# Two blocks' attention results turned on PE and ACT, and an earlier due time for the first weights in the order

## The chip, the cores and the metric

The kernel runs on one core of one Trainium2 chip. The metric is the device time of one execution in microseconds (us), the median of several executions. Engines, as the profile names them: PE is TensorE (matmuls and transposes; PEld is its weight load), DVE is VectorE, ACT is ScalarE, POOL is GpSimd, and SP is SyncE, which here only issues transfers (DMAs). Each engine runs its own list of instructions strictly in order and waits on semaphores for the others. The lists are fixed when the program is built.

## The reference

Chunked attention on 4 batches, 8 heads and 768 tokens, then a mixture of 8 experts whose mixing weights are balanced by eight Sinkhorn rounds:

```python
for c in range(nc):                       # 24 chunks of 32 queries
    # keys: 8 memory keys, and the chunk with 16 before and 8 behind it
    scores = scale * q_c @ k_full.T
    a = exp(scores - max(scores)); a = a / (sum(a) + 1e-9)
    out[:, :, chunk] = a @ v_full
x = out.transpose(0, 2, 1, 3).reshape(3072, 512)
logits = x @ w_gate; P = exp(logits - logits.max())
for _ in range(8):
    P /= P.sum(1) + 1e-9;  P /= P.sum(0) + 1e-9;  P *= N / E
for e in range(8):
    out += P[:, e] * (maximum(x @ w1[e], 0) @ w2[e])    # w1: 512x1024, w2: 1024x512
```

## The kernel before

Attention and experts are one program. The 3072 tokens are cut into 24 **blocks** of 128 tokens; attention works block by block, and two blocks make one of the groups of 256 tokens on which the expert matmuls run. For block n, `scores` has PE turn queries and keys (tq L1014, tk L1018, tx L814 for the rest of the context's keys), multiply them (sp L1077), DVE take the row maximum and subtract it (sm L1091, s L1097) and ACT the exponential (s L1116). `values` has PE turn the exponentials (ta L1134), ACT copy them to SBUF (at L1153), and PE multiply them with the values (xp L1144; the values carry a column of ones, so the row sum comes along). Then DVE divides (`share`: rec L1162 and L1163, xq L1165 twice), and turns the result so that features lie on the partitions (`turn_out`, STREAM_TRANSPOSE L1185, in squares of 32 by 32). The turned result xg is the input x of the experts.

The expert matmuls are done with pairs of 16-bit numbers. Every operand is scaled by a power of two that is found from its largest magnitude, and split into a high part (ACT, L518) and the rest (DVE, L526). So before the first expert matmul can start there is a **chain of scales**: the maxima of the values for x (vmax L982) and of the weights (mxs L562) on DVE, most_of L450, a transpose on PE (row_x and row_w, L499), a few tiny instructions on DVE (L507, L455, L456), PE again (sp_x, sp_w L486), DVE again (sx, sw L462), and then the splits. The first expert's first-layer weights w1f come in four tiles of 512 KB (`fetch_first`, `load` L553), the second layer's w2f too. The first unit of work uses plain products (pp L2046 for the first layer, yp L2127 for the second, h L2088 between them); all later ones use a Strassen form with sums of operands (px, py, pz, yx, yy, yz at L1599; the sums ws L606 and xt L1291 to L1315 on POOL or DVE; the intermediate sums c at L1668).

**What sets the order.** Every piece of work is a `Task` with an engine, a cost and a due time. `Plan` runs a list schedule over all of them when the program is built: it keeps a clock for each engine, takes the task that can start first, and emits its instructions in that order. A transfer is counted as landed at the end of its share of a common transfer clock, plus 2.6. So the numbers of the plan decide only the order; the chip then waits for what really comes last. Where the plan thinks that PE would be idle for more than 0.4 us it puts in matmuls without a result, named **warm** (L432, each 128x256), about as many as fill 0.8 of the gap. PSUM is cut into banks in groups ("att", "two", "main" and others); a task that `takes` a bank waits in the plan until one of its group is free.

## Time and profile before

| | |
|---|---|
| median of 3 runs | 1910.08 us (1908.98 to 1910.18) |
| profiled execution | 1910.83 us |
| its span in the trace | 1908.8 us |
| PE busy | 1898.1 us (99%) |
| DVE busy | 1466.2 us (77%) |
| ACT busy | 1022.9 us (54%) |
| POOL busy | 541.4 us (28%) |
| granted PE clock | 1.00 |

The profiled execution took 2.0 us more than its span, the time around it. In the views below a row of the timeline has the start, the length (of the whole group, where several are merged), the engine, the line, the operation, what it writes and reads, and in brackets how long the engine sat idle before it and who ended that. A row of the windows view has a stretch, its length, and for each engine its busy time and number of instructions.

### The profile page before, as it was taken

Reading aid. Unit: us, or ns where it says so; the run is one execution under the profiler, and the core shown is the slowest. Engines: PE = TensorE matmul, PEld = TensorE weight load, DVE = VectorE, ACT = ScalarE, POOL = GpSimd, SP = SyncE. Lnnn points to the kernel's source line nnn. Section 1 sums busy time; section 2 is a strip of 40 time slices with the busy share of each in tenths; the row PEclk is TensorE's granted clock in tenths of the full one; section 3 lists DMA queues with packets and bytes.
Section 4 is the critical chain, followed back from the end, with each engine's and each line's share of the span. In section 5 each row is a group of like instructions: output and inputs, shape, how many; then the busy total and the mean of one; then the engine's idle time right before and its main releaser. Section 6 shows DMA issues by size and latency. Waiting matters only on the chain.

```text
span 1908.8 us, 47094 instructions
## 1 busy us (share of the span) xinstructions
PE 1898.1 (99%) x19544; PEld 1635.1 (86%) x19544; DVE 1466.2 (77%) x2456; ACT 1022.9 (54%) x1999; POOL 541.4 (28%) x605
## 2 busy tenths in 40 slices
PE   9999999999999999999999999999999999999999
PEld 7777676788888888888888888888888888888888
DVE  6886679878589867898669876897778985786565
ACT  4765555556465545546445544655555563564453
POOL 4321112513134211522224231442124231332112
PEclk9999999999999999999999999999999999999999
DMA  9887653543324441264224433245313632322321
GB/s 212 199 217 167 169 168 126 168 166 106 128 78 161 150 142 70 90 222 160 84 95 160 156 122 112 89 160 183 123 45 115 247 109 100 95 84 85 127 84 67
DMA packets 207254, 254.81 MB, mean 133 GB/s; under 512 B 106208, under 2 KB 140128, under 8 KB 202688
## 3 DMA queue, kind: packets, MB, share of 16 engines
q1 hardware_dynamic: 203044, 249.17, 40.7%
q0 software_dynamic: 2080, 2.18, 0.6%
q8 instruction: 153, 2.51, 0.6%
q10 hardware_dynamic: 1916, 0.46, 0.2%
q14 instruction: 61, 0.50, 0.1%
HBM read 187.84 MB, written 63.44 MB: 132 GB/s over the span
## 4 chain that ended last, share of the span: by engine, by line
PE 97%; DVE 2%; issue 0%; ACT 0%; POOL 0%; DVEq 0%; POOLq 0%; ACTq 0%
PE px L1599 26%; PE yx L1599 23%; PE pz L1599 13%; PE yz L1599 11%; PE py L1599 6%; PE yp L2127 6%; PE yy L1599 6%; PE pp L2046 1%; PE xp L1144 1%; PE sp L1077 1%; PE warm L432 1%; PE ta L1134 1%; PE tk L1018 1%; PE tq L1014 0%; DVE w L526 0%; PE lp L1400 0%
## 5 line engine op out<-in xcount | busy, mean ns | idle before, releaser
L1599 PEld LDWEIGHTS <-w 128*128 128x128 f16 x7896 | 771.3, 98 | 93.9 <-issue 2.1
L1599 PEld LDWEIGHTS <-h 128*128 128x128 f16 x7056 | 690.4, 98 | 81.1 <-issue 0.9
L1599 PE MATMUL px<-x,w 128*128 128x256 f16 x4512 | 548.3, 273 | 0.6 <-DVE c L1668 0.5
L1932 POOL TENSOR_TENSOR acc<-acc,y 128x256 f32<-128x256 f32 x252 | 263.7, 1054 | 879.1 <-ACT y L1907 866.4
L1599 PE MATMUL yx<-w,h 128*128 128x256 f16 x4032 | 467.9, 273 | 0.5 <-DVE acc L1942 0.5
L1658 ACT ACTIVATE q<-px 128x256 f32<-128x256 f32 x376 | 143.1, 382 | 289.1 <-PE px L1599 284.2
L1599 PE MATMUL pz<-x,w 128*128 128x256 f16 x2256 | 278.1, 273 | 0.0
L1599 PE MATMUL yz<-w,h 128*128 128x256 f16 x2016 | 233.8, 273 | 0.0
L1827 DVE TENSOR_TENSOR h<-ss,h 128x1024 f16<-128x1024 f32 x168 | 217.7, 1299 | 3.6 <-ACT h L1803 3.6
L1778 ACT ACTIVATE h<-c 128x768 f16<-128x768 f32 x168 | 140.8, 838 | 111.6 <-DVE c L1668 111.6
L1803 ACT CAST h<-ss 128x1024 f16<-128x1024 f32 x168 | 174.1, 1039 | 38.5 <-DVE ss L1767 38.5
L1767 DVE SCALAR_TENSOR_TENSOR ss<-c,ss 128x256 f32<-128x256 f32 x336 | 176.4, 525 | 8.6
L1811 DVE SCALAR_TENSOR_TENSOR h<-c,h 128x768 f16<-128x768 f32 x168 | 168.2, 1004 | 9.2 <-ACT h L1778 9.1
L1668 DVE SCALAR_TENSOR_TENSOR c<-px,q 128x256 f32<-128x256 f32 x188 | 77.7, 421 | 96.6 <-PE px L1599 90.7
L1907 ACT ACTIVATE y<-yx,pscale 128x256 f32<-128x256 f32 x168 | 79.6, 474 | 120.6 <-PE yx L1599 116.5
L1599 PE MATMUL py<-x,w 128*128 128x256 f16 x1128 | 139.0, 273 | 0.6 <-DVE c L1668 0.6
L2127 PE MATMUL yp<-w,h 128*128 128x512 f16 x576 | 132.2, 379 | 0.5 <-DVE h L2088 0.5
L1767 DVE SCALAR_TENSOR_TENSOR ss<-c,h 128x512 f32<-128x512 f32 x168 | 125.0, 744 | 1.9 <-ACT h L1755 1.9
L1668 DVE SCALAR_TENSOR_TENSOR c<-py,q 128x256 f32<-128x256 f32 x188 | 78.4, 421 | 61.1 <-PE py L1599 56.5
L1599 PE MATMUL yy<-w,h 128*128 128x256 f16 x1008 | 116.9, 273 | 0.0
L2127 PEld LDWEIGHTS <-h 128*128 128x128 f16 x576 | 55.5, 99 | 58.9 <-DVE h L2088 1.0
L518 ACT ACTIVATE w<-ws,sw 128x1024 f16<-128x1024 f32 (+1 forms) x64 | 69.4, 1089 | 65.6 <-POOL ws L606 65.5
(165 smaller groups left out, 1775.1 us busy)
## 6 DMA issues: line engine op xcount, KB each, us to landing
x<-xkeep SPq DMA_DIRECT2D x28, 1792.0 KB
akeep<-acc SPq DMA_DIRECT2D x168, 256.0 KB
acc<-akeep SPq DMA_DIRECT2D x168, 256.0 KB
w1f<-in_moe_w_dram SPq DMA_DIRECT2D x36, 512.0 KB
w2f<-in_moe_w_dram SPq DMA_DIRECT2D x32, 512.0 KB
w1fm<-in_moe_w_dram SPq DMA_DIRECT2D x28, 512.0 KB
w2fm<-in_moe_w_dram SPq DMA_DIRECT2D x28, 512.0 KB
xkeep<-x SPq DMA_DIRECT2D x6, 1792.0 KB
```

The costliest lines, as they stand in the source:

```text
L518: lambda: nc.scalar.activation(dst(0), src(), AF.Copy, scale=s),
L1599: nc.tensor.matmul(dst.t, a, b, start=(not more and n == 0), stop=(n == end), skip_group_check=more,)
L1658: lambda: nc.scalar.activation(t.t, src.t, AF.Copy, scale=DOWN),
L1668: lambda: nc.vector.scalar_tensor_tensor(c.t[:, o], src.t, DOWN, q.t, op0=ALU.mult, op1=ALU.add),
L1767: lambda: nc.vector.scalar_tensor_tensor(dst(), src(), 0.0, other(), op0=ALU.max, op1=op),
L1778: lambda: nc.scalar.activation(h.t[:, 0, 0:3], c.t, AF.Relu),
L1803: lambda: nc.scalar.copy(h.t[:, 0, 3:7], ss.t),
L1811: lambda: nc.vector.scalar_tensor_tensor(h.t[:, 1, 0:3].rearrange("p a n -> p (a n)"), c.t.rearrange("p a n -> p (a n)"), 0.0, h.t[:, 0, 0 ...
L1827: lambda: spare.tensor_tensor(h.t[:, 1, 3:7], ss.t, h.t[:, 0, 3:7], op=ALU.subtract),
L1907: (lambda: nc.scalar.activation(t.t, src.t, AF.Copy, scale=f))
L1932: lambda: nc.gpsimd.tensor_tensor(acc.t[:, cols], acc.t[:, cols], q.t, op=ALU.add),
L2127: nc.tensor.matmul(py.t, hf.t[:, hl, where[fh], o : o + P], room(fp, WIDE * wl + DM * fh, WIDE * wl + DM * (fh + 1)), start=(fp == 0 and i ...
```

## The change

Two things. First, for blocks 0 and 1 the turn is moved from DVE to PE and ACT: `share` writes xq in another layout (the multiply is of the form 128x4x4x16 in place of 128x16x16, still twice), PE does four 128x128 transposes into a bank of the group "att" (xt), and ACT copies them to xg. For xq to come out so, xp is written with chunk and head pair exchanged. All other blocks stay as they were. Second, a task can have a `lead`, which is taken off the landing time that the plan counts for its transfer; the four loads of w1f have 3.8, all others 0.

```diff
+LEAD = 3.8
...
-                t.end = max(dma, at + t.cost) + 2.6
+                t.end = max(dma, at + t.cost) + 2.6 - t.lead
...
-        return st, add(eng, 1, go, after, prio, [st], dma=2.1)
+        return st, add(eng, 1, go, after, prio, [st], dma=2.1, lead=lead)
...
+        by_pe = n < 2
...
+                        m, j = (c, i) if by_pe else (i, c)
                         nc.tensor.matmul(
-                            xp.t[i * CH : (i + 1) * CH, par, c * DV : (c + 1) * DV],
+                            xp.t[m * CH : (m + 1) * CH, par, j * DV : (j + 1) * DV],
...
-        xq = buf("at", att, [P, CB, KT, CH], F32, f"xq_{n}")
+        xq = buf("at", att, [P, KT, P] if by_pe else [P, CB, KT, CH], F32, f"xq_{n}")
...
+                if by_pe:
+                    nc.vector.tensor_tensor(
+                        xq.t.rearrange("p k (i a f) -> p i k a f", a=2, i=HP)[:, :, :, a],
+                        x[:, a, :, 0:D].rearrange("p i (f k) -> p i k f", k=KT),
+                        r[:, a, :, None, None].broadcast_to([P, HP, KT, D // KT]),
+                        op=ALU.mult,
+                    )
+                    continue
...
-        t = add("DVE", 0.73, turn_out, [t], at + 2, [xq, gt])
+        if by_pe:
+            tx = bank("att", [P, KT, QB], f"xt_{n}")
+
+            def go_x():
+                for i in range(KT):
+                    nc.tensor.transpose(tx.t[:, i], xq.t[:, i], ident)
+
+            t = add("PE", 0.5, go_x, [t], at + 2, [xq, gt], takes=tx)
+            t = add(
+                "ACT",
+                0.6,
+                lambda: nc.scalar.copy(gt.t[:, :, o : o + QB], tx.t),
+                [t],
+                at + 2,
+                [gt],
+                frees=tx,
+            )
+        else:
+            t = add("DVE", 0.73, turn_out, [t], at + 2, [xq, gt])
...
-            st, ld = load(0, fp, which, FIRST[which - 1] + 0.5 * fp)
+            st, ld = load(0, fp, which, FIRST[which - 1] + 0.5 * fp, lead=LEAD if which == 1 else 0.0)
```

Since the plan schedules all tasks together, both edits move far more than the two blocks. Apart from line numbers and buffer numbers, the orders differ from the start up to work that ran at about 190 us before, and are the same from there on: the last 2024 of some 2270 rows of DVE, the last 30120 of some 32040 of PE, the last 1773 of ACT, 527 of POOL and 536 of SP agree. SP's first 54 rows, with the loads of w1f among them, agree too.

The first place is DVE at the start, from its first vmax to the last maximum of w1f. Blocks 0 and 1 are the first and second group of rec, xq; names end in a buffer's number. Before:

```order
L982 TENSOR_REDUCE vmax<-v_pair 128x1
L1162 TENSOR_SCALAR rec_425<-xp_390 128x8
L1163 RECIPROCAL rec_425<-rec_425 128x8
L1165 TENSOR_TENSOR xq_428<-xp_390,rec_425 128x16x16 x2
L1185 STREAM_TRANSPOSE xg_471<-xq_428 128x4x128
L1091 TENSOR_REDUCE sm_474<-sp_436 128x2x4
L1097 TENSOR_TENSOR s_477<-sp_436,sm_474 128x2x4x64
L982 TENSOR_REDUCE vmax<-v_pair 128x1
L562 TENSOR_REDUCE mxs<-w1f_0_290 128x1
L562 TENSOR_REDUCE mxs<-w1f_1_330 128x1
L1162 TENSOR_SCALAR rec_559<-xp_524 128x8
L1163 RECIPROCAL rec_559<-rec_559 128x8
```

After:

```order
L983 TENSOR_REDUCE vmax<-v_pair 128x1
L563 TENSOR_REDUCE mxs<-w1f_0_290 128x1
L1166 TENSOR_SCALAR rec_464<-xp_390 128x8
L1167 RECIPROCAL rec_464<-rec_464 128x8
L1170 TENSOR_TENSOR xq_467<-xp_390,rec_464 128x4x4x16 x2
L1092 TENSOR_REDUCE sm_473<-sp_431 128x2x4
L1098 TENSOR_TENSOR s_485<-sp_431,sm_473 128x2x4x64
L983 TENSOR_REDUCE vmax<-v_pair 128x1
L563 TENSOR_REDUCE mxs<-w1f_1_330 128x1
L563 TENSOR_REDUCE mxs<-w1f_2_340 128x1
L1166 TENSOR_SCALAR rec_559<-xp_524 128x8
L1167 RECIPROCAL rec_559<-rec_559 128x8
```

The maximum of w1f's first tile now stands ahead of block 0's rec, so DVE can't begin to divide block 0's result until that tile has landed; the other maxima stand earlier too, three of the four ahead of block 1's rec, and both STREAM_TRANSPOSE rows are gone.

The second place is DVE where the first Strassen unit begins (in the trace of before from 104 to 115 us): x is the unit's input split, w_0_2 and w_0_3 are the last two weight tiles' splits, c the unit's first intermediate sums, s the scores of a later block. Before:

```order
L526 SCALAR_TENSOR_TENSOR x_1996<-xg_1795,sx,x_1996 128x256
L526 SCALAR_TENSOR_TENSOR x_1996<-xt_1_2013,sx,x_1996 128x4x256
L526 SCALAR_TENSOR_TENSOR w_0_2_685<-ws_0_2_1884,sw,w_0_2_685 128x768
L1668 SCALAR_TENSOR_TENSOR c_1_0_2096<-py_1_0_2085,q_0_1_0_2072 128x256
L1097 TENSOR_TENSOR s_2100<-sp_1936,sm_1986 128x2x4x64
L1431 COPY lg<-lq_1975 128x32
L1668 SCALAR_TENSOR_TENSOR c_1_1_2119<-py_1_1_2102,q_0_1_1_2077 128x256
L562 TENSOR_REDUCE mxs<-w1fm_0_1835 128x1
L1091 TENSOR_REDUCE sm_2171<-sp_2121 128x2x4
L1097 TENSOR_TENSOR s_2184<-sp_2121,sm_2171 128x2x4x64
L526 SCALAR_TENSOR_TENSOR w_0_3_750<-ws_0_3_2098,sw,w_0_3_750 128x256
L1668 SCALAR_TENSOR_TENSOR c_1_0_2096<-px_1_0_2055,q_0_1_0_2197 128x256
```

After:

```order
L527 SCALAR_TENSOR_TENSOR x_2023<-xg_1827,sx,x_2023 128x256
L527 SCALAR_TENSOR_TENSOR x_2023<-xg_1462,sx,x_2023 128x256 x2
L527 SCALAR_TENSOR_TENSOR x_2023<-xg_1827,sx,x_2023 128x256
L527 SCALAR_TENSOR_TENSOR w_0_3_751<-ws_0_3_2017,sw,w_0_3_751 128x256
L527 SCALAR_TENSOR_TENSOR w_0_3_751<-ws_0_3_2017,sw,w_0_3_751 128x768
L1098 TENSOR_TENSOR s_2108<-sp_1930,sm_1967 128x2x4x64
L527 SCALAR_TENSOR_TENSOR x_2023<-xt_0_2019,sx,x_2023 128x4x256
L1698 SCALAR_TENSOR_TENSOR c_1_0_2124<-py_1_0_2095,q_0_1_0_2093 128x256
L1461 COPY lg<-lq_2002 128x32
L527 SCALAR_TENSOR_TENSOR x_2023<-xt_1_2082,sx,x_2023 128x4x256
L1698 SCALAR_TENSOR_TENSOR c_1_1_2189<-py_1_1_2110,q_0_1_1_2103 128x256
L1092 TENSOR_REDUCE sm_2199<-sp_2149 128x2x4
```

The two splits of w_0_3 and the scores s have moved ahead of the split of the sum xt_0, and that split ahead of the unit's first c on DVE; before, w_0_3 stood behind the first maximum w1fm.

The third place is POOL ahead of the same unit: the sums ws of the weight tile w_0_3 and the sums xt of the unit's input. Before:

```order
L606 TENSOR_TENSOR ws_0_2_1884<-w1f_2_1336,ws_0_2_1884 128x256
L798 DMA kx_1811<-in_k_dram 32x8x64
L1299 TENSOR_TENSOR xt_0_1993<-xg_1795 128x256
L1291 TENSOR_TENSOR xt_1_2013<-xg_1795,xg_1432 128x256
L1299 TENSOR_TENSOR xt_1_2013<-xg_1795 128x256
L1307 TENSOR_TENSOR xt_1_2013<-xg_1795,xt_1_2013 128x256
L1315 TENSOR_TENSOR xt_1_2013<-xg_1432,xt_1_2013 128x256
L606 TENSOR_TENSOR ws_0_3_2098<-w1f_3_1453 128x256
L606 TENSOR_TENSOR ws_0_3_2098<-ws_0_3_2098,w1f_3_1453 128x256
L606 TENSOR_TENSOR ws_0_3_2098<-w1f_3_1453 128x256
L606 TENSOR_TENSOR ws_0_3_2098<-w1f_3_1453,ws_0_3_2098 128x256
```

After:

```order
L607 TENSOR_TENSOR ws_0_2_1900<-ws_0_2_1900,w1f_2_1322 128x256
L607 TENSOR_TENSOR ws_0_2_1900<-w1f_2_1322 128x256
L607 TENSOR_TENSOR ws_0_2_1900<-w1f_2_1322,ws_0_2_1900 128x256
L607 TENSOR_TENSOR ws_0_3_2017<-w1f_3_1459 128x256
L607 TENSOR_TENSOR ws_0_3_2017<-ws_0_3_2017,w1f_3_1459 128x256
L607 TENSOR_TENSOR ws_0_3_2017<-w1f_3_1459 128x256
L607 TENSOR_TENSOR ws_0_3_2017<-w1f_3_1459,ws_0_3_2017 128x256
L1329 TENSOR_TENSOR xt_0_2019<-xg_1827 128x256
L1321 TENSOR_TENSOR xt_1_2082<-xg_1827,xg_1462 128x256
L1329 TENSOR_TENSOR xt_1_2082<-xg_1827 128x256
L1337 TENSOR_TENSOR xt_1_2082<-xg_1827,xt_1_2082 128x256
L1345 TENSOR_TENSOR xt_1_2082<-xg_1462,xt_1_2082 128x256
```

The four sums of w_0_3 went ahead of the sums xt; before they came behind them.

On PE the rows that count are the warm matmuls. Up to the first pp there are 168 of them before and 139 after; between the first pp and the first yp 19 before and 32 after; around the start of the first Strassen unit 5 before, and after 13 ahead of its first px and 14 behind its second py; none later in either. The eight transposes of xt stand in PE's order behind block 0's and block 1's xp, and tq and tk of block 2 have moved from between row_w and sp_w to behind sp_w. In the stretch ahead of the first yp, the maxima of the last three w2f tiles on DVE stand behind h of the first two tiles (before, behind none or one), and all four h ahead of the first w2 split; before, only three h stood ahead of it, and the last one came 16 rows behind the third, after all four w2 splits.

More of the change, by code (lines that the diff above doesn't have):

```diff
@@ L30 @@
 FAR = 60.0
+LEAD = 3.8
 class Task:
-    __slots__ = ("eng", "cost", "fn", "prio", "left", "ready", "end", "then", "takes", "frees", "n", "dma", "start", "many")
+    __slots__ = ("eng", "cost", "fn", "prio", "left", "ready", "end", "then", "takes", "frees", "n", "dma", "start", "many", "lead")
 class Past:
@@ L105, in __init__, with add @@
         self.again = 0.0
-    def add(self, eng, cost, fn, deps=(), prio=0.0, bufs=(), takes=None, frees=None, dma=0.0, many=False):
+    def add(self, eng, cost, fn, deps=(), prio=0.0, bufs=(), takes=None, frees=None, dma=0.0, many=False, lead=0.0):
         t = Task()
@@ L110, in add @@
         t.ready, t.end, t.then, t.n, t.dma = 0.0, None, [], len(self.tasks), dma
-        t.many = many
+        t.many, t.lead = many, lead
         if dma:
@@ L539, in tile_chunked_attn_sinkhorn_moe, with load @@
     known = {}
-    def load(e, fp, which, prio, ahead="", eng="SP", after=()):
+    def load(e, fp, which, prio, ahead="", eng="SP", after=(), lead=0.0):
         shape = [P, KT, 2, P] if which == 1 else [P, 2, DM]
```

## The prediction

> **What bounds the kernel now.** I read the page's head and engine table first, then the chain of work that ended last.
>
> ```profile
> span 1908.8 us, 47094 instructions
> PE 1898.1 (99%) x19544; PEld 1635.1 (86%) x19544; DVE 1466.2 (77%) x2456; ACT 1022.9 (54%) x1999; POOL 541.4 (28%) x605
> PE 97%; DVE 2%; issue 0%; ACT 0%; POOL 0%; DVEq 0%; POOLq 0%; ACTq 0%
> ```
>
> PE is the bound nearly everywhere. So a change can gain only where PE idles or runs matmuls without a result. The windows view, by stages of the program, and the same view for the warm matmuls alone say where that is:
>
> ```profile
> core 0: us, PE busy (x) PEld busy (x) DVE busy (x) ACT busy (x) POOL busy (x), PEclk, DMA share, GB/s
> 0.00:36.00 36.00, 31.77 (x473) 25.30 (x474) 17.84 (x40) 12.29 (x24) 20.53 (x39) 1.00 1.02 195
> 36.00:50.00 14.00, 14.00 (x240) 12.18 (x239) 13.90 (x22) 11.08 (x25) 2.80 (x5) 1.00 1.05 245
> 50.00:70.00 20.00, 18.76 (x441) 12.96 (x439) 18.98 (x37) 15.26 (x27) 7.26 (x6) 1.00 0.67 147
> 98.00:114.00 16.00, 15.23 (x246) 10.77 (x246) 13.77 (x28) 11.35 (x24) 6.38 (x9) 1.00 1.00 280
> 114.00:200.00 86.00, 85.99 (x1541) 63.68 (x1541) 64.91 (x124) 49.27 (x102) 16.87 (x28) 1.00 0.68 164
> ...
> 0.00:36.00 36.00, 22.84 (x168) 1.00 1.02 195
> 50.00:70.00 20.00, 2.59 (x19) 1.00 0.67 147
> 98.00:114.00 16.00, 0.71 (x5) 1.00 1.00 280
> ```
>
> Three stages have slack. Up to 36 us PE waits for the first operands (idle, or warm). From 50 to 70 us it idles 20.00 - 18.76 = 1.24 us, from 98 to 114 us 0.77 us. From 114 to 200 us it idles 0.01 us. Everything that is won or lost must be settled in these stages, since from about 190 us on the orders are the same and PE is full: nothing behind can take a delay up, and nothing can lose a gain. What DVE does late in the program is off the path.
>
> **Start-up: the chain through DVE.** The timeline of DVE, from block 0's first vmax to the maxima that open the chain of scales, and the first pp on PE:
>
> ```profile
> 15.68 1.22 DVE L982 TENSOR_REDUCE vmax<-v_pair 128x1 f32<-128x1024 f32 x1 [0.27 <-DMA v_pair<-in_v_dram]
> 19.22 0.17 DVE L1162 TENSOR_SCALAR rec<-xp 128x8 f32<-128x8 f32 x1 [2.32 <-PE xp L1144]
> 19.72 0.75 DVE L1165 TENSOR_TENSOR xq<-xp,rec 128x256 f32<-128x256 f32 x2
> 20.51 0.71 DVE L1185 STREAM_TRANSPOSE xg<-xq 128x512 f32<-128x512 f32 x1
> 21.15 0.65 DVE L1091 TENSOR_REDUCE sm<-sp 128x8 f32<-128x512 f32 x1
> 22.44 1.21 DVE L982 TENSOR_REDUCE vmax<-v_pair 128x1 f32<-128x1024 f32 x1
> 23.57 2.34 DVE L562 TENSOR_REDUCE mxs<-w1f 128x1 f32<-128x1024 f32 x2
> 26.40 0.17 DVE L1162 TENSOR_SCALAR rec<-xp 128x8 f32<-128x8 f32 x1 [0.49 <-PE xp L1144]
> 26.91 0.76 DVE L1165 TENSOR_TENSOR xq<-xp,rec 128x256 f32<-128x256 f32 x2
> 27.69 0.71 DVE L1185 STREAM_TRANSPOSE xg<-xq 128x512 f32<-128x512 f32 x1
> 28.33 2.30 DVE L562 TENSOR_REDUCE mxs<-w1f 128x1 f32<-128x1024 f32 x2
> 30.55 0.14 DVE L450 TENSOR_REDUCE most_of<-vmax 128x1 f32<-128x2 f32 x1
> ...
> 35.68 2.56 PE L2046 MATMUL pp<-x,w 128*128 128x256 f16 x22
> ```
>
> A STREAM_TRANSPOSE costs DVE 0.64 us from start to start (20.51 to 21.15, 27.69 to 28.33), so 1.28 us for both. That is the first edit's whole saving on DVE. In its place come four transposes and an ACT copy, as in these rows of the same forms:
>
> ```profile
> 23.24 0.65 PE L1134 MATMUL ta<-ident,s 128*128 128x128 f32 x4 [0.61 <-ACT s L1116]
> 23.98 0.59 ACT L1153 COPY at<-ta 128x512 f32<-128x512 f32 x1 [0.80 <-PE ta L1134]
> ```
>
> About 0.65 and 0.59 us for each block. PE only waits there and ACT is free, and x is needed two steps of the chain of scales later, so I cost them at nothing; without that cover they would be 1.2 us on block 1. The multiply's new form 128x4x4x16 is in no row. The old form's pair costs 0.75 us (19.72); I bound the new one by half of that and by twice, so by -0.4 and +0.75 us for each block, and take the old price, the nearest row, since elements and memories are the same.
>
> The second edit puts the first maximum of w1f ahead of block 0's rec. DVE was idle there from 16.90 to 19.22, so at 1.13 us for a maximum (22.44 to 23.57 from start to start, for the same form) it is free only if the tile has landed by 18.1. The view doesn't give the landing of w1f; these rows of the transfers (issue of w1f, bytes moved in slices of 0.4 us from 12 to 28 us, and a small load of POOL in the same stretch with its us to landing) bound it:
>
> ```profile
> L553 SPq DMA_DIRECT2D w1f<-in_moe_w_dram x4: 622/642/653, 13.0 to 15.2; - x4
> GB/s 302 203 137 134 145 143 126 185 200 129 154 159 248 343 369 307 241 348 382 316 262 228 312 376 382 388 374 340 329 300 241 214 161 174 176 158 123 195 142 142
> kx<-in_k_dram POOLq DMA_DIRECT2D x2, 64.0 KB, 6.3
> ```
>
> The rate rises above 300 only from 17.2 us on (slice 14), which I read as w1f's long rows reaching the front of the queue behind the many short rows issued ahead of them. From there 0.5 MB have passed at 18.8 us if all of it is w1f (343 + 369 + 307 + 241 GB/s over 0.4 us each). The other end is 23.57 us, where DVE began the maximum in the profile with no wait. A 64 KB load takes 6.3 us, and 13.0 + 0.6 + 6.3 = 19.9. I estimate the landing at 20.2, between the ends and nearest to that row. So this new wait takes the place of the old one, and ends later. What is queued behind it on DVE is block 0's rec, then the scores of block 1, and for these wait ACT's exponential, PE's ta and xp, and block 1's rec:
>
> - maximum from 20.2, 1.13 us: rec of block 0 at 21.35 instead of 19.22.
> - from rec to the second vmax 22.44 - 19.22 - 0.64 = 2.58 without the transpose: 23.93.
> - from there to block 1's rec 26.40 - 22.44 = 3.96 (exponential, ta, at, xp): 27.89. DVE's own work in that time, a vmax and two maxima, is 3 x 1.13 = 3.4 and fits.
> - rec and xq 27.69 - 26.40 = 1.29: 29.18; the one maximum that is left 1.11: most_of at 30.29.
>
> Against 30.55 that is **-0.3 us**. Both transposes' 1.28 us and the moved maxima are almost wholly eaten by the wait. In general most_of comes 10.1 us after the landing: at 18.8 the term is -1.7, at 23.5 it is +3.0.
>
> [...]
>
> **50 to 70 us, and 98 to 114 us: matmuls without a result.** The waits of PE in these stages, and the warm groups:
>
> ```profile
> 53.20 0.35 PE L486 MATMUL sp_w<-most_of,one 1*128 1x1 f32 x2 [0.41 <-DVE most_of L456]
> 55.14 1.48 PE L432 MATMUL warm<-ident 128*128 128x256 bf16 x12
> 56.92 0.85 PE L1144 MATMUL xp<-w,at 64*32 64x65 f32 x64 [0.29 <-DMA x_room<-in_v_dram]
> 68.31 1.04 PE L2127 MATMUL yp<-w,h 128*128 128x512 f16 x4 [0.54 <-DVE h L2088]
> 108.36 0.71 PE L432 MATMUL warm<-ident 128*128 128x256 bf16 x5
> 108.90 0.82 PE L1599 MATMUL py<-x,w 128*128 128x256 f16 x6
> 110.30 0.81 PE L1599 MATMUL py<-x,w 128*128 128x256 f16 x6 [0.58 <-DVE c L1668]
> ```
>
> 0.41 + 0.29 + 0.54 = 1.24 is the whole idle time of the stage from 50 us. A warm matmul holds PE for 0.11 us ((108.90 - 108.36) / 5). It stands in PE's list, so it costs its 0.11 us whether or not the chip has a gap there. Before, 24 of them stand behind the first pp: 2.6 us. After, 32 + 13 + 14 = 59: 6.5 us. That is **+3.85 us**, and the largest term. It is the plan's own estimate of the gaps that the new order opens: the Strassen unit's input waits behind weight sums on POOL and weight splits on DVE. DVE, busy 13.77 of 16 us there, has no room to take this up.
>
> Two waits of before go. h of the last tile, for which yp waited 0.54 us at 68.31, now stands ahead of the w2 splits: **-0.54**. The 0.58 us at 110.30, a wait for the unit's c on DVE, falls where 14 warm matmuls (1.5 us) now stand ahead of the same kind of work: **-0.58**. The rest, 0.41 and 0.29 us, I leave. New idle time of PE beside the warm ones I take as nothing; its bounds are -0.7 (the rest covered too) and +1.5 (half of the 27 warm matmuls' 2.97 us again, if the plan sees that gap a third too small).
>
> **Sum.** -0.3 + 3.85 - 0.54 - 0.58 = **+2.4 us**. Made against the profiled execution that is 1910.8 + 2.4 = 1913.2 (its span 1908.8 and 2.0 around it); it lies 0.75 us above the median shown, so I give 1910.1 + 2.4 = 1912.5 for the median. A measurement of this kernel tells no change from a change of about 0.2%, 3.8 us; so the likeliest is "the same", on the slow side.
>
> **The rivals.**
>
> 1. *The tile lands early*, as the plan now believes. Then rec of block 0 stays at 19.22, its successors come at 21.80, 25.76 and 28.16: most_of 2.4 us sooner, and the total is +2.4 - 2.1 = +0.3, 1910.4. For it: DVE is idle until 19.22 anyway, and any landing up to 18.1 does it. Against it: the rate rises only from 17.2 us on. Chance 0.15.
> 2. *The tile lands late*: slower. The mechanism is the same wait, its price 1 us for 1 us of landing. The total passes +3.8 from a landing at 20.2 + 1.4 = 21.6 us on; at 23.5 it is +5.7, 1915.8. For it: w1f's four tiles are 2.1 MB, which at 300 to 390 GB/s from 17.2 us last until 23.6, and if the queues share them out evenly the first ends near the last. Against it: they were issued one after the other over 2.2 us. Chance 0.20; unforeseen waits of PE in the Strassen unit would add to it.
> 3. *The gaps were there before*: faster. If the new order's warm matmuls stand only in time that PE would lose anyway, then behind the first pp 6.5 us of warm replace all of the 24 warm and the 2.01 us idle (2.6 + 2.01 = 4.65): +1.85 and no less. With an early tile, -2.4, and without the wait in this row, which goes because tq and tk no longer stand between row_w and sp_w on PE:
>
> ```profile
> 33.05 0.16 DVE L461 TENSOR_SCALAR uw<-sp_w 128x1 f32<-128x1 f32 x1 [0.54 <-PE sp_w L486]
> ```
>
> the splits start 0.54 us sooner still, and the total is 1.85 - 2.4 - 0.54 = -1.1, 1909.0. It decides only if all three hold. In the forecast I leave the 0.54 out, since the high parts on ACT wait for sx and not for this. A gain of over 3.8 us would need a further cause that I don't see. Chance 0.07.
>
> The forecast has 0.58.
>
> **How the numbers follow.** Forecast, 1912.5. Range: from 1908.0, 1 us below rival 3, to 1916.3, rival 2 at its bound of 23.5 with half a us of other waits. Faster by over 0.2%: 0.07, rival 3 with a cause that I don't see. Slower by over 0.2%: rival 2's 0.20 and 0.05 of the forecast's own upper end (new idle of 1.5): 0.25. The same: 0.68.
>
> **What would show it.** On DVE a wait ahead of the first mxs for the transfer of w1f that ends near 20.2 us, and no wait of rec for xp; most_of at about 30.3; first pp within 0.5 us of 35.4. Warm groups of 32 between first pp and first yp, and of 13 and 14 near 110 us, with PE's idle time from 50 to 70 us near 0.7 and little around 110. No wait for h near 68 us. The same PE rows from 190 us on, shifted by +2.4. I am wrong if the first mxs starts near 17 or 23 us, or if PE idles over 1 us beside the warm groups near 110 us.

## The result, and the profile after

| | before | after |
|---|---|---|
| median, 6 runs each | 1909.89 us (1908.83 to 1911.82) | 1919.57 us (1918.89 to 1921.32) |
| profiled execution | 1910.83 us | 1919.03 us |
| its span | 1908.8 us | 1917.0 us |
| PE busy | 1898.1 us | 1901.7 us |

The ratio is 1.0051, with a 95% interval of 1.0040 to 1.0061: the change makes the kernel slower by half a per cent, more than twice what a measurement of it can tell from no change. The profiled executions differ by 8.2 us, the medians by 9.7.

The head, the engine table and the chain of waits of the changed kernel's page, and then its windows by stage (stretch, length, busy time and instructions of each engine, granted PE clock, DMA share, GB/s):

```profile
span 1917.0 us, 47119 instructions
PE 1901.7 (99%) x19558; PEld 1637.8 (85%) x19558; DVE 1469.4 (77%) x2454; ACT 1024.4 (53%) x2001; POOL 540.3 (28%) x605
PE 96%; DVE 2%; DMA 1%; issue 0%; ACT 0%; SPq 0%; ACTq 0%; DVEq 0%
```

```profile
50.00:70.00 20.00, 19.63 (x355) 13.03 (x343) 17.02 (x33) 13.41 (x25) 6.31 (x6) 1.00 0.75 171
70.00:98.00 28.00, 27.02 (x548) 20.30 (x548) 22.05 (x40) 18.23 (x38) 10.48 (x16) 1.00 0.99 247
98.00:116.00 18.00, 14.77 (x221) 10.37 (x221) 16.54 (x26) 11.05 (x22) 8.64 (x11) 1.00 0.57 162
...
170.00:176.20 6.20, 4.37 (x90) 3.12 (x89) 1.14 (x3) 2.68 (x7) 0.00 (x0) 1.00 1.03 243
176.20:179.60 3.40, 3.40 (x18) 2.45 (x17) 1.00 (x2) 1.29 (x3) 0.00 (x0) 0.50 0.62 153
```

PE's busy time grew by 3.6 us, the span by 8.2, so more than half of the loss is PE standing still. The windows say where: 0.98 us from 70 to 98 us (none before), 3.23 us from 98 to 116 us (0.77 before), 1.83 us from 170 to 176 us (none before). And for 3.4 us behind that the clock is 0.50, which costs half of the window, 1.7 us, though PE counts as busy. The same stages in PE's timeline of the changed kernel:

```profile
75.78 0.85 PE L1078 MATMUL sp<-kC,qT 64*32 64x64 f32 x64 [0.98 <-DVE xq L1177]
...
105.78 1.58 PE L433 MATMUL warm<-ident 128*128 128x256 bf16 x13
...
109.48 1.03 PE L1629 MATMUL px<-x,w 128*128 128x256 f16 x8 [1.69 <-DVE x L527]
110.35 1.47 PE L1629 MATMUL py<-x,w 128*128 128x256 f16 x12
113.14 1.69 PE L433 MATMUL warm<-ident 128*128 128x256 bf16 x14 [1.31 <-DVE s L1098]
115.06 0.63 PE L1135 MATMUL ta<-ident,s 128*128 128x128 f32 x4 [0.23 <-ACT kC L1029]
...
175.06 0.24 PE L1078 MATMUL sp<-kC,qT 64*32 64x64 f32 x1 [1.83 <-issue]
175.90 2.45 PE L1629 MATMUL px<-x,w 128*128 128x256 f16 x12
```

Three things are to be read. In the Strassen unit the 13 and 14 warm matmuls are there as the plan put them, and PE waits beside them still: 1.69 us for a split x on DVE, and 1.31 us in front of a warm matmul itself, which needs the PSUM bank that DVE's s has yet to free. At 175.06 the 64th matmul of a group of 64 equal ones comes 1.83 us late and the view names no releaser: in this view PE waited for nothing. And the twelve px behind it take 2.45 us where twelve py took 1.47 at full clock. The start, on DVE:

```profile
19.08 1.22 DVE L563 TENSOR_REDUCE mxs<-w1f 128x1 f32<-128x1024 f32 x1 [2.52 <-DMA w1f<-in_moe_w_dram]
...
20.71 0.75 DVE L1170 TENSOR_TENSOR xq<-xp,rec 128x256 f32<-128x256 f32 x2
...
28.73 0.14 DVE L451 TENSOR_REDUCE most_of<-vmax 128x1 f32<-128x2 f32 x1
```

The wait moved as foreseen, from block 0's xp to the first tile of w1f, and ended at 19.08. Here the first pp starts at 33.70 instead of 35.68. So the start gained, and the rest lost more:

| stage | foreseen | in the profile |
|---|---|---|
| first pp | -0.3 | -2.0 (33.70 - 35.68) |
| warm matmuls behind it, 59 for 24 | +3.85 | +3.85 |
| idle from 50 to 70 us | -0.54 | -0.87 (0.37 - 1.24) |
| sp at 75.78 | 0 | +0.98 |
| idle at the Strassen unit, 98 to 116 us | -0.58 | +2.46 (3.23 - 0.77) |
| sp at 175.06 | 0 | +1.83 |
| PE at half clock behind it | 0 | +1.7 |
| sum | +2.4 | +7.95 of 8.2 |

Why DVE comes so late in the Strassen unit shows when its instructions are grouped by shape in the same stretch, 95 to 118 us (line, form, count | busy us, mean ns | idle before). Before, and then after:

```profile
L526 DVE SCALAR_TENSOR_TENSOR x<-xg,sx,x 128x256 f16<-128x256 f32 x6 | 2.6, 479 | 0.2 <-ACT x L518 0.2
L1291 DVE TENSOR_TENSOR xt<-xg,xg 128x256 f32<-128x256 f32 x1 | 0.4, 406 | 0.0
```

```profile
L527 DVE SCALAR_TENSOR_TENSOR x<-xg,sx,x 128x256 f16<-128x256 f32 x6 | 5.4, 944 | 0.0
L1321 DVE TENSOR_TENSOR xt<-xg,xg 128x256 f32<-128x256 f32 x1 | 0.9, 901 | 0.0
```

The same six splits of the same shape take 944 ns where they took 479. What differs is their neighbour. POOL's timeline after, across the splits that DVE makes from 105.02 to 111.1:

```profile
103.22 0.73 POOL L607 TENSOR_TENSOR ws<-w1f 128x256 f32<-128x256 f32 x1 [4.09 <-DVE ux L462]
...
105.64 0.91 POOL L607 TENSOR_TENSOR ws<-w1f,ws 128x256 f32<-128x256 f32 x1
```

Before, POOL's sums xt were done at 101.6 and POOL then sat idle until 109.38, so DVE had the time alone:

```profile
100.83 0.80 POOL L1315 TENSOR_TENSOR xt<-xg,xt 128x256 f32<-128x256 f32 x1
109.38 0.72 POOL L606 TENSOR_TENSOR ws<-w1f 128x256 f32<-128x256 f32 x1 [7.76 <-ACT q L1658]
```

In the new order the sum ws_0_3 of weights stands ahead of xt on POOL and waits there 4.09 us. The view names DVE's ux, which ends at 103.21; the kernel has one buffer for ws, and DVE's splits of w_0_2 that read it end just ahead of that, at 103.14. So nine sums now run beside DVE's splits, and both become slower, POOL's from 0.73 to 0.91 us.

### The profile page after: what moved, and what is told of

The parts are those of the page before. It is cut to its first block, busy times and chain, and to the rows that moved or that the text cites. A ratio compares the mean times of both kernels' runs of the same rounds, so it can differ in the third digit from the quotient of the medians.

```text
span 1917.0 us, 47119 instructions
## 1 busy us (share of the span) xinstructions
PE 1901.7 (99%) x19558; PEld 1637.8 (85%) x19558; DVE 1469.4 (77%) x2454; ACT 1024.4 (53%) x2001; POOL 540.3 (28%) x605
## 3 DMA queue, kind: packets, MB, share of 16 engines
q10 hardware_dynamic: 1916, 0.46, 0.1%
## 4 chain that ended last, share of the span: by engine, by line
PE 96%; DVE 2%; DMA 1%; issue 0%; ACT 0%; SPq 0%; ACTq 0%; DVEq 0%
PE px L1629 26%; PE yx L1629 23%; PE pz L1629 13%; PE yz L1629 11%; PE py L1629 6%; PE yp L2157 6%; PE yy L1629 6%; PE xp L1148 1%; PE pp L2076 1%; PE sp L1078 1%; PE tq L1015 1%; PE ta L1135 1%; DVE x L527 1%; PE tk L1019 0%; DMA v_pair<-in_v_dram 0%; PE warm L433 0%
```

## The experiments

The first four take the change apart, and separate three causes: the operations of the turn, the re-made order, and the warm matmuls as a plain cost.

**Both edits without the re-made order.** The transposes and the copy are issued inside the one DVE task of before, and the first maximum of w1f is issued ahead of block 0's rec by hand, so that the plan's tasks stand as before.

```diff
-LEAD = 3.8
+LEAD = 0.0
...
+            if n == 0:
+                firsts[0]()
...
-            t = add("PE", 0.5, go_x, [t], at + 2, [xq, gt], takes=tx)
...
+            t = add("DVE", 0.73, turn_pe, [t], at + 2, [xq, gt], takes=tx, frees=tx)
```

> Both edits at their own place, but the rest in the order of before: DVE does the maxima of w1f in the places that they have after (one tile earlier each, the first ahead of block 0's rec), PE and ACT turn blocks 0 and 1, and every other row of every engine, the warm matmuls too, stands as before. Theory A (the two edits gain at the start, and the re-made order behind them loses more): first pp near 33.7 us as after, no new waits of PE behind it, time 1907.5 to 1908.5 us, 1.5 to 2.5 below before. Rival B (the edits themselves cost, by the wait for the landing or by operands that come earlier than their transfers): first pp gains, but waits on transfers grow behind it, 1911 us or more. Rival C (a start that is earlier by 2 us is eaten before 60 us by the w2 chain): 1909.5 to 1910.5 us.

Measured: 1914.71 us (1913.56 to 1917.29) against 1909.44, ratio 1.0029 (1.0017 to 1.0040). The first pp came at 38.47, later than in any other kernel here. PE's timeline of it, and then one row of DVE's:

```profile
29.11 0.66 PE L1215 MATMUL xt<-ident,xq 128*128 128x128 f32 x4 [1.40 <-DVE xq L1178]
29.60 4.09 PE L433 MATMUL warm<-ident 128*128 128x256 bf16 x36
```

```profile
33.84 0.28 DVE L508 TENSOR_REDUCE most_of<-row_x 1x1 f32<-1x128 f32 x1 [3.47 <-PE row_x L500]
```

None of the expectations held. The 36 warm matmuls filled a gap of PE ahead of row_x; with the transposes put in front of them they can start only when block 1's xq is there, and then they themselves stand in the way for 4 us. It says nothing on the turn's price, but what a list of warm matmuls does when the work ahead of it moves: it becomes the path.

**The 59 warm matmuls behind the first pp left out**, everything else as in the changed kernel.

```diff
+            warmed[0] += 1
+            if warmed[0] <= 139:
-            nc.tensor.matmul(wp, idle[:, 0:P], idle, start=True, stop=True)
+                nc.tensor.matmul(wp, idle[:, 0:P], idle, start=True, stop=True)
```

> The changed kernel without the 59 warm matmuls behind the first pp; its other rows are the same. If a warm matmul always costs its 0.11 us, as the prediction had it, 6.5 us less: 1913 us. Theory A: most of them stand where PE waits anyway (13 ahead of a px that still waits 1.69 us, 27 ahead of sp_w and sp), so only some 1 to 2.4 us go: 1917 to 1918.5 us. Rival D (the warm matmuls keep the clock up): with 2 to 3 us of idle time in a row near 110 us the granted clock halves for a few us there, and the time is the same or longer, 1919.5 to 1922 us.

Measured: 1919.74 us (1919.27 to 1921.08), ratio 1.0054 (1.0042 to 1.0067), the same as with them, as rival D had it. Its PE timeline at the Strassen unit, and windows of 3.4 us ahead of and behind two of its waits (PE busy, granted clock, DMA share, GB/s):

```profile
112.14 1.03 PE L1632 MATMUL px<-x,w 128*128 128x256 f16 x8 [2.98 <-DVE x L530]
...
117.72 0.66 PE L1138 MATMUL ta<-ident,s 128*128 128x128 f32 x2 [3.24 <-ACT kC L1032]
```

```profile
49.30:52.70 3.40, 1.70 (x71) 1.00 0.84 173
52.70:59.50 6.80, 5.70 (x79) 0.50 0.50 98
...
114.20:117.60 3.40, 0.28 (x3) 1.00 0.12 43
117.60:121.00 3.40, 3.28 (x74) 0.50 0.47 198
```

The waits at the unit became 2.98 + 3.24 = 6.22 us. With the warm matmuls there were 3.23 us of waits and 27 x 0.11 = 2.97 us of warm: 6.20 us. So the new order's gap at this place is 6.2 us, whether it is filled or not, where it was 0.77 + 5 x 0.11 = 1.3 before. The plan had filled half of it. The other 32 warm matmuls (3.5 us) are saved, and the stall and half clock at 175 us (3.5) are gone too. Against that, in the profile, the clock is 0.50 while PE works for 5.70 + 3.28 us, which loses half of it, 4.5 us; PE waits 2.0 us instead of 0.4 from 50 to 53 us, and 0.8 us more ahead of the sp at 56.28; and w1f landed 1.0 us later in this execution. That is +0.9 by terms, and the spans differ by 0.5.

**The turn alone, and the earlier landing alone.** In the first only `LEAD` is 0, in the second only `by_pe` is False.

```diff
-LEAD = 3.8
+LEAD = 0.0
```

> The turn on PE and ACT alone, the plan counting w1f as before (no lead); the plan makes its own order. It has 57 warm matmuls behind the first pp against 24 before and 59 after. Theory A: a start earlier by about 1.3 us (two transposes off DVE), and a re-made order that loses as after: 1913 to 1919 us. Rival B2 (the lead is what spoils the order): 1908 to 1910 us.

```diff
-        by_pe = n < 2
+        by_pe = False
```

> The lead alone, all blocks turned by DVE; the plan makes its own order, with 67 warm matmuls behind the first pp. Theory A: start earlier by at most 1 us, re-made order that loses: 1913 to 1920 us. Rival B3 (the turn on PE is what spoils the order): 1908 to 1910 us.

Measured: the turn alone 1913.74 us (1913.17 to 1914.37), ratio 1.0022 (1.0013 to 1.0032); the landing alone 1916.26 (1914.86 to 1916.47), ratio 1.0033 (1.0020 to 1.0045), both in the range of their theory A. Either edit re-makes the order by itself, and in both orders the warm matmuls behind the first pp are many, 57 and 67 for 24. The waits that are left in the stages behind, in PE's timeline of the turn alone:

```profile
77.56 0.85 PE L1078 MATMUL sp<-kC,qT 64*32 64x64 f32 x64 [0.97 <-DVE xq L1177]
...
109.07 3.11 PE L433 MATMUL warm<-ident 128*128 128x256 bf16 x27
```

PE does not wait in the Strassen unit there, there is no late 64th matmul and no half clock. The loss in it is mainly 33 more warm matmuls (3.6 us) and the 0.97 us at the sp, less a first pp 1.0 us earlier (34.70). With the landing alone the first pp is not earlier at all (36.12 in its profile), 43 more warm matmuls stand behind it (4.7 us), and the sp waits 1.03 us. Both orders lose by themselves (4.3 and 6.8 us), and the whole (9.7 in the medians) is not their sum: it has waits at the unit and a stall that the turn's order hasn't.

The second group asks how steady the late 64th matmul is, what the place of an instruction in PE's list does to it, and whether POOL's late sums are the cause at the unit.

**The changed kernel again**, without an edit.

> The changed kernel once more, to see which of its waits come again in another execution. Theory E (PE's 1.83 us stall inside sp at 173 us belongs to the place of the instructions, since the profile names no releaser for it and one 16 KB load of instructions starts beside it): the stall comes again within 0.5 us, the clock is 0.50 for 3.4 us behind it, 1919 to 1921 us. Rival F (a chance meeting with transfers): no stall there in this profile, or one of another length, and a span shorter by 3 us.

Measured: 1919.67 us (1917.59 to 1923.07), ratio 1.0051 (1.0037 to 1.0064). The profiled execution was the slowest, 1923.07. PE's timeline and windows of it:

```profile
22.79 1.11 PE L1207 MATMUL xt<-ident,xq 128*128 128x128 f32 x4 [2.79 <-DVE xq L1170]
...
178.93 0.24 PE L1078 MATMUL sp<-kC,qT 64*32 64x64 f32 x1 [2.09 <-issue]
```

```profile
18.60:22.00 3.40, 1.40 (x69) 1.00 1.09 340
22.00:28.80 6.80, 6.01 (x44) 0.50 1.04 218
```

The stall stands in front of the same 64th matmul, 2.09 us now, with the half clock behind it, as theory E had it. The waits of the unit are the same to 0.02 us (1.67, 1.32, 0.23). What is new is half clock at the start: PE waited 2.79 us for block 0's xq, which stands behind the wait for w1f, and ran at 0.50 from 22.0 to 28.8 us. The first pp came at 37.22. The early maximum makes this possible: whatever follows it on PE waits for the landing too. With the turn alone PE waited 0.26 us at this place, and with the landing alone 2.70 us, in front of a ta.

The half clock is not in every execution. Of the changed kernel's ten on record, four have a mean granted clock of 1.000, and took 1917.59 to 1919.38 us; the other six have 0.997 to 0.999, and took 1919.03 to 1923.07. So the four still lost 7.7 us or more, and the 1.7 us of a half clock count in full in the profiled executions, but not in every execution behind the median.

**Twenty early warm matmuls fewer**, which moves all later PE instructions 40 places up its list (a matmul is two, weights and data: the profile's page counts 19558 of PE and 19558 of PEld).

```diff
+            if not (34 <= k < 44 or 102 <= k < 112):
-            nc.tensor.matmul(wp, idle[:, 0:P], idle, start=True, stop=True)
+                nc.tensor.matmul(wp, idle[:, 0:P], idle, start=True, stop=True)
```

> The changed kernel without 20 of the warm matmuls ahead of the first pp, in two groups of ten at places where PE waits anyway; every other row is the same, but all rows behind stand 40 instructions earlier in PE's program. Theory E: the boundary between two loads of instructions then falls 40 instructions later, behind sp and among matmuls of 273 ns, so the stall at 173 us and the half clock behind it go: 3.5 us less, 1916 us. Rival F: the stall has nothing to do with the place; 1919 to 1920 us as after.

Measured: 1918.89 us (1918.21 to 1919.74), ratio 1.0045 (1.0033 to 1.0058), 0.8 us below the changed kernel beside it. The stall of the 64th matmul was gone, but waits of PE without a releaser stood ahead of two other matmuls (0.51 us ahead of 177.75, 0.25 ahead of 259.72), one of 1.49 us for DVE's c ahead of 1050.27, and at the start the clock was 0.50 from 21.7 to 25.1 us. Counted from the start, the one at 177.75 is at the old place in the list: 2880 matmuls are ahead of it, as ahead of the late one in both profiles of the changed kernel, but now a pz stands there. So the stall keeps its place in the list, and the work moves past it. Neither range held (1916 us, or 1919 to 1920), and the experiment doesn't give the stall's price: inconclusive on that.

**POOL's sum ws_0_3 behind xt**, by a time before which the plan doesn't issue it.

```diff
+            if (e, fp, which) == (0, 3, 1):
+                sums[0].ready = 111.8
```

> The changed kernel, with one number more in the plan: the sums ws_0_3 on POOL may not start before 111.8 of the plan's clock, so that they stand behind the sums xt as before. The plan is the same up to there, and has 13 + 4 + 5 warm matmuls around the first Strassen unit in place of 13 + 14. Theory A2 (the sums of w_0_3 ahead of xt, and the splits of w_0_3 that come with them on DVE, delay the unit's input): the waits of 1.69 and 1.31 us near 110 us shrink to under 1 us together, and with 5 warm matmuls less 2 to 3 us go; 1916.5 to 1917.5 us, and 3.5 us less again if the stall at 173 us goes with the shift of the rows. Rival G (the unit's input is late because the blocks ahead of it are late): the waits stay, 1919 us.

Measured: 1913.01 us (1911.39 to 1916.04, 11 runs), ratio 1.0017 (1.0008 to 1.0025), **6.7 us below the changed kernel** on the same chip, as theory A2 had it for a stall that goes too. Its DVE groups by shape in the same stretch, and PE's timeline:

```profile
L527 DVE SCALAR_TENSOR_TENSOR x<-xg,sx,x 128x256 f16<-128x256 f32 x6 | 3.1, 552 | 0.0
...
L1323 DVE TENSOR_TENSOR xt<-xg,xg 128x256 f32<-128x256 f32 x1 | 0.9, 902 | 0.0
```

```profile
108.40 1.03 PE L1631 MATMUL px<-x,w 128*128 128x256 f16 x8 [0.75 <-DVE x L527]
```

Here only ws_0_3's four sums, from 103.55 to 106.9 us, lie beside DVE. DVE's xt of 103.65 lies in that stretch and still takes 902 ns; the four splits that follow it from 107.08 are at full speed, 1.66 us for all four, and the mean falls to 552. Both conditions stand in one execution: slow beside POOL, fast without. The unit's waits fell from 3.23 to 0.75 us, and five warm matmuls fell away (0.55). Not all of that is POOL as a neighbour: the edit re-made DVE's order too, and the splits of w_0_3 (1.40 us in the changed kernel) and one split x now stand behind the scores s. The px's wait, 1.69 to 0.75 us, is the neighbour's, since the same four splits stand ahead of it in both; the 1.54 us in front of the warm matmul and of ta went by both. The rest of the 6.7 is the stall and the half clock at 175 us (3.5), which are gone in this execution, with ten places fewer ahead of them on PE's list.

**The first experiment with fewer warm matmuls**, since they had been in the way: 11, 31 and 10 of three groups are left out.

```diff
+            if not (91 <= k < 102 or 112 <= k < 143 or 158 <= k < 168):
-            nc.tensor.matmul(wp, idle[:, 0:P], idle, start=True, stop=True)
+                nc.tensor.matmul(wp, idle[:, 0:P], idle, start=True, stop=True)
```

> As both_old_order, without the warm matmuls that there stood behind the moved transposes and held row_x up by 3.47 us: 10 of 21 kept ahead of ta, 5 of 36 ahead of row_x, 15 of 25 ahead of the first pp. Theory A (the edits gain at the start, and the order behind them decides the rest): first pp at 34 to 35 us, and 0.7 to 1.7 us less than before in the end, 1907.8 to 1908.8 us. Rival B (an earlier start only runs into later waits): 1909.5 us or more though the first pp is earlier.

Measured: 1913.58 us (1911.64 to 1915.82, 11 runs), ratio 1.0018 (1.0009 to 1.0027). By the number this is rival B. The first pp came at 34.24, though xt waited 2.37 us for xq and the clock was 0.50 from 22.5 to 25.9. Idle time of 1.64 us (3.40 - 1.76) between 87.4 and 90.8 was followed by half clock too:

```profile
87.40:90.80 3.40, 1.76 (x71) 1.00 0.81 204
90.80:94.20 3.40, 3.40 (x16) 0.50 0.76 181
```

That the missing warm matmuls let the clock fall is not shown here: the wait of 2.37 us (1.62 with all of them) ends ahead of the first group of which some were left out, and the idle time from 87.4 us on lies behind the first pp, where no warm matmul was left out.

The third group puts warm matmuls where PE waits at the start, and makes the best kernel that these readings suggest.

**The same number of warm matmuls, 14 of them moved** to places where PE waits near 20 us; once in the changed kernel, once with ws_0_3 behind xt as well. A table says how often each of the program's warm matmuls is issued:

```diff
+TIMES = {37: 0, 38: 0, 39: 0, 40: 0, 41: 0, 42: 0, 43: 0, 83: 12, 94: 4, 105: 0, 106: 0, 107: 0, 108: 0, 109: 0, 110: 0, 111: 0}
...
+            for _ in range(TIMES.get(k, 1)):
+                nc.tensor.matmul(wp, idle[:, 0:P], idle, start=True, stop=True)
```

> The changed kernel with as many warm matmuls, 14 of them moved: 7 of the first 44 and 7 of 12 ahead of block 1's xt go, 11 more stand ahead of block 0's xt and 3 more behind it, so that PE has work while it waits for xq near 20 us. All rows from the first pp on keep their places. Theory H (PE's waits of 1.4 to 2.4 us near 20 us halve the clock in some executions): the clock is 1.00 up to 170 us in this profile, the first pp is at 33.5 to 35 us, and the median falls by 0.5 to 1.5 us against the changed kernel, to 1918 to 1919 us; the stall inside sp near 173 us and the half clock behind it come again. Rival I (the half clock at the start is of no account, or comes anyway): 1919.5 us as before, or a half clock near 22 us in the profile.

> after_sums_later with the same 14 warm matmuls moved. Its own profile had no half clock, and a time 1.5 us below its median of 1913.0 us. Theory H: that median is spoilt by the half clock near 22 us in other executions; without it 1911 to 1912 us. Rival I: 1913 us. What is left above before (1909.8 us) is the wait of 1.0 us near 75 us, that of 0.75 us near 107 us and 30 more warm matmuls, against an earlier start of 2 us.

Measured: 1920.27 us (1917.72 to 1920.58), ratio 1.0050 (1.0036 to 1.0064), and 1913.07 us (1911.97 to 1913.60, 11 runs), ratio 1.0016 (1.0007 to 1.0025). The profiled executions show no half clock at the start (granted clock 1.000 in all 11 runs of the second, which spread over 1.6 us instead of 4.7), but neither median is better, as rival I had it: the half clock at the start makes single executions slow, not the median. In the first the 64th matmul was late once more, by 1.93 us.

**The turn alone with nothing else moved against it**: the tasks as before, the transposes issued at two chosen warm matmuls, no maximum ahead of block 0's rec, three of them ahead of block 1's, and the warm matmuls moved to the waits.

```diff
+TIMES = {72: 5, 80: 3, 106: 2, 97: 0, 98: 0, 99: 0, 100: 0, 101: 0, 137: 0, 138: 0, 139: 0, 140: 0, 141: 0, 142: 0}
...
+                for i in ((0,), (1, 2), (3,), ())[k]:
+                    firsts[i]()
...
+                held[(83, 127)[n]] = go_x
```

> The turn on PE and ACT in the order of before, without the early maximum: DVE divides block 0's result when it comes (near 19.2 us), and three maxima of w1f stand between the second vmax and block 1's rec. Warm matmuls are moved so that PE has work where it waits for xq. Theory A (the edits gain at the start where nothing waits for a landing, and the order behind the start decides the rest): first pp at 33.5 to 34.5 us, all waits behind it as before, 1.0 to 2.0 us less than before, 1907.9 to 1908.9 us. Rival B (an earlier start only runs into later waits, or into half clocks): first pp earlier, but 1909.5 us or more.

Measured: 1909.78 us (1908.38 to 1911.18, 11 runs) against 1910.28, ratio 0.9999 (0.9990 to 1.0007): the best kernel of the study, 0.5% below the changed one, and not to be told from before. Rows of its DVE timeline, and of PE's:

```profile
28.16 0.14 DVE L460 TENSOR_REDUCE most_of<-vmax 128x1 f32<-128x2 f32 x1
```

```profile
33.68 3.44 PE L2091 MATMUL pp<-x,w 128*128 128x256 f16 x30
...
98.27 0.30 PE L1098 MATMUL sp<-kC,qT 64*32 64x64 f32 x2 [0.31 <-issue]
...
170.65 0.41 PE L1098 MATMUL sp<-kC,qT 64*32 64x64 f32 x19 [0.91 <-issue]
```

In the profile the turn brings what it can, most_of 2.4 us and the first pp 2.0 us earlier than before. Of this, 0.31 + 0.91 us go in new waits without a releaser, again inside sp, and the span is 0.8 us shorter. In the medians even that isn't seen, so theory A's 1907.9 to 1908.9 us were missed, and rival B holds.

**Ten places fewer.** The kernel with 14 moved warm matmuls, and five of the first warm matmuls left out: ten instructions fewer ahead of the 64th matmul, as in the kernel with ws_0_3 behind xt, but POOL's order as in the changed kernel.

```diff
-TIMES = {37: 0, 38: 0, 39: 0, 40: 0,
+TIMES = {32: 0, 33: 0, 34: 0, 35: 0, 36: 0, 37: 0, 38: 0, 39: 0, 40: 0,
```

> after_warm_spread with 5 warm matmuls less among the very first (PE's first 32 in place of 37, where it waits for the first transfers), so that every later row of PE stands 10 instructions earlier in its program and nothing else changes. Theory E (the stall of 1.8 to 2.1 us ahead of the 64th matmul of sp near 174 us, three times in three profiles, belongs to the place of that instruction in the program, as where one load of instructions ends, and the half clock follows from the stall): both are gone from that place, and with no other stall in their stead 3.5 us less than after_warm_spread's 1920.3, 1916 to 1917.5 us; 1918 us where a stall of another place takes a part back. Rival F (it belongs to the work, say to the transfers that SP issues there): stall and half clock stay, 1919.5 to 1920.5 us.

Measured: 1916.60 us (1915.11 to 1917.66) against 1909.64, ratio 1.0035 (1.0021 to 1.0049). PE's timeline of the kernel with the 14 moved, and of this one, at the same group of sp:

```profile
176.10 0.24 PE L1087 MATMUL sp<-kC,qT 64*32 64x64 f32 x1 [1.93 <-issue]
```

```profile
112.01 1.03 PE L1638 MATMUL px<-x,w 128*128 128x256 f16 x8 [1.67 <-DVE x L536]
...
174.91 0.86 PE L1087 MATMUL sp<-kC,qT 64*32 64x64 f32 x64
```

The stall and its half clock are gone, as theory E had it, the median is 3.7 us lower (3.0 when each is set against the kernel before on its own chip), and the unit's waits (1.67, 1.32) are as they were. So the two causes are apart: POOL's sums ahead of xt, which run beside DVE's splits, make the waits at 109 us, and the position in PE's list makes the stall at 175 us. On the scale of the profile the part of the first that moving ws_0_3 removed is worth 3.0 us (2.5 of waits and 0.5 of warm), the second 3.5: together 6.5 of the 6.7 that moving it gave.

## Why the prediction was wrong

The forecast was 1912.5 us with a range to 1916.3; measured were 1919.57. The side was the forecast's own, slower, and the chance of 0.68 stood on "the same".

- **The wait for w1f: right.** It took the place of the wait for xp. Estimated landing 20.2; in eight profiles with this order DVE began the first maximum between 18.77 and 21.62 us, 19.95 in the mean.
- **What follows the landing: right in kind, 0.45 us too long.** most_of came 28.73 - 19.08 = 9.65 us behind it where 10.1 was worked out, and the first pp 14.6 to 14.8 us behind it in the six of these profiles without half clock at the start (33.70 - 19.08; 36.24 - 21.62 with the latest landing). With the mean landing the first pp is at 34.6, 1.1 us earlier than before instead of 0.3; the profile of after, with -2.0, is one of the early ones. The kernel without an early maximum had most_of at 28.16, so the lead bought nothing at the start.
- **The new multiply: right**, 0.75 us for the pair, the price of the old form. **The transposes and the copy at nothing: right**; from most_of to the first pp are 4.97 us, and were 5.13.
- **The warm matmuls, +3.85: right as a count, too simple as a cost.** Without them the time was the same. They stood in the new order's gaps, and held the clock: without them it was 0.50 from 52.7 to 59.5 and from 117.6 to 121.0 us, with them 1.00 there.
- **The two waits of before: one right, one wrong.** h is no longer waited for. The -0.58 at the unit didn't come: that wait was replaced by longer ones.
- **The step that failed** is this one: "New idle time of PE beside the warm ones I take as nothing; its bounds are -0.7 (the rest covered too) and +1.5 (half of the 27 warm matmuls' 2.97 us again, if the plan sees that gap a third too small)." It was 0.98 + 3.23 + 1.83 us, and 1.7 us of half clock behind the last. So the term that was put at nothing, with 1.5 us as its upper bound, was 6.0 us, and 7.7 with the half clock. Two parts of it have different causes.

The first part could have been seen in advance. The order showed the weight sums ahead of xt on POOL and the splits behind them on DVE, and the prediction named that place. But the plan prices such a split at 0.53 us on DVE whatever POOL does, and the prediction took the plan's gap over without a price of its own; alone it takes 0.48 us, beside POOL's sums 0.94. The trace of before has a pair of rows that shows it, the same form of a split w once beside POOL's sums xt and once with POOL idle:

```profile
99.98 1.06 DVE L526 SCALAR_TENSOR_TENSOR w<-ws,sw,w 128x256 f16<-128x256 f32 x1
...
114.38 0.47 DVE L526 SCALAR_TENSOR_TENSOR w<-ws,sw,w 128x256 f16<-128x256 f32 x1
```

Other rows agree: x<-xg,sx,x and xt<-xg,xg took 0.90 to 0.94 us beside POOL's sums in the changed kernel and 0.41 to 0.48 with POOL idle in the one before, and where POOL's sums were moved away four splits took 1.66 us together. By what means the two engines slow each other, the runs don't show. The prediction had looked at PE, DVE and ACT, and at POOL only for when its results come.

The second part, the stall in front of one matmul of sp, was no rival. Yet before has a smaller one of the kind in PE's timeline, at the start, which I had not read as what it is:

```profile
25.62 0.72 PE L1144 MATMUL xp<-v_pair,at 64*32 64x65 f32 x48 [0.64 <-issue]
```

That is 0.64 us inside a run of 64 small matmuls, again without a releaser. That the one at 175 us hangs on the place in PE's list is shown: it came in front of the same matmul in three executions (1.83, 2.09, 1.93 us) and not in the kernels with 10, 40 or 118 places fewer ahead of it; with 40 fewer it kept its place behind 2880 matmuls (0.51 us). The 0.16 us of before at 100.78 and the 0.31 us at 98.27 in the turn alone with nothing moved against it stand at one place too, behind 1739 matmuls. In the view of the transfers of the changed kernel, from 170 to 178 us, the queue that loads instructions is at work (packets, MB, share of 16 engines):

```profile
q8 instruction: 2, 0.03, 2.1%
```

Two packets of 16 KB passed there, while the DMA engines were full (share 1.03 in the windows above). The records of these packets say more. The changed kernel has 153 of them for the 39,116 matmuls and weight loads of PE, 256 to a packet in the mean. The timelines show ten waits of PE without a releaser, 0.16 to 2.09 us long. Each of the four in the profiles of before and after ended 1.34 to 1.57 us after such a packet had landed: in the changed kernel it landed at 173.68 and PE went on at 175.06, in the one before at 17.26, 24.28 and 99.21, and PE went on at 18.78, 25.62 and 100.78. So I take it that PE waited for its next instructions; only these times speak for it. Why those loads came late isn't shown.

- **The rivals.** Rival 2 had the right sign and the nearest size (+5.7), with another cause: its own size needed a landing at 23.5, and the eight landings lay between 18.8 and 21.6, the last of them where the rival was to begin. "Unforeseen waits of PE in the Strassen unit", which it named in passing, was the larger matter. Rival 3's condition, that the warm matmuls stand only in time that PE would lose anyway, held at the unit, but for a gap that the change itself had opened.
- **What would show it wrong** was put down rightly: "if PE idles over 1 us beside the warm groups near 110 us". It idled 3.2.

Open: the sp at 75.78, 0.98 us behind DVE's xq, which is 0.96 to 1.10 us in all ten profiles of orders that either edit or both re-made, was not taken apart. Nor were the 3 us that remain with ws_0_3 behind xt: 30 more warm matmuls (3.3 us) account for it in number, but without warm matmuls the clock fell.

## What to carry to other kernels

When a scheduler re-makes an order, read on each engine not only what stands ahead of what, but which engines now work at the same time, and price each operation from rows with the same neighbour: DVE's split x, beside POOL's sums, took 944 ns instead of 479. Matmuls without a result are no plain cost: take them away only together with the gap that they fill, or the clock can take the saving back (4.5 us of it here, at 0.50). And a local gain of 2 us in a program of 19,500 matmuls can be lost because everything behind it moved a few places in its list, so a difference of 0.2% is judged only after the list has been shifted by some harmless instructions.

## What the runs showed of the hardware

**Half clock followed some waits of PE.** A drop to 0.50 lasted 3.41 us in the changed kernel (176.21 to 179.62), and 6.8 us at the start of its second profile (22.0 to 28.8). In the 3.4 us ahead of four drops PE had been idle for about half of the time or more, and not for all of it: 1.64 of 3.40 us (87.4 to 90.8), 1.70 of 3.40 (49.3 to 52.7), 2.00 of 3.40 (18.6 to 22.0), 3.12 of 3.40 (114.2 to 117.6), in the rows above. Such idle time was not always followed by a drop: not the 1.67 us ahead of the px at 113.09 in the changed kernel's second profile (1.00 from 98 to 120 us), nor the 1.69 us ahead of the one at 109.48 in its first (1.00 from 98 to 116). What decides it isn't shown. A drop of 3.41 us costs up to 1.7 us, by an estimate of half its length.

**DVE and POOL started by turns.** From 105 to 110 us in the changed kernel both start an instruction every 0.87 us (DVE at 105.02, 105.88, 106.75; POOL at 104.77, 105.64, 106.51), alternately. In the kernel before, DVE's form took 0.48 us with POOL idle, and POOL started one every 0.69 us (110.19, 110.87, 111.56).

**A matmul waited up to 2.09 us without a releaser in the view**, at places that came again: behind 2880 matmuls (1.83, 2.09, 1.93 and 0.51 us) and behind 1739 (0.16 and 0.31 us). Eight of the ten such waits in the timelines lie inside a run of 64 small matmuls of about 13 ns each (0.86 us for 64). The one at 175 us cost 3.5 us in the profile with the half clock that followed. The four in the profiles of before and after ended 1.34 to 1.57 us behind the landing of a 16 KB packet of instructions; behind the other 302 landings of such packets in these two profiles PE shows no such wait.
